# Attention decode with a gated FFN on one core: value loop split per batch, scores moved between transposes, output products in four column groups

## The chip, the core and the metric

One core of a Trainium2 chip runs the whole kernel in one launch. The metric is the device time of that launch in microseconds (us), measured outside the profile; a run's number is the median of several executions. A profile is one further execution with its own time, and its clock starts at zero at the first recorded instruction.

## The reference

Two sequences (B = 2) each decode one token of width 512. The attention part has 32 heads of 128 and a cache of 4096 keys and values per head. A dense two-layer part with 1376 hidden units runs beside it on its own input, and a gate mixes the two results:

```python
q = (x @ wq).reshape(B, 1, 32, 128)               # per head
scores = einsum("bhqd,bhkd->bhqk", q, k) * 128 ** -0.5
p = softmax(scores)
a = (einsum("bhqk,bhkd->bhqd", p, v)).reshape(B, 1, 4096) @ wo
b = relu(B_x @ w1) @ w2
g = sigmoid((x * gate_w).sum(-1))
out = g * a + (1 - g) * b                         # 2 x 512
```

Everything is bf16. The key cache and the value cache are 64 MiB each and every element is used once, so nearly all the bytes that the kernel moves are these two.

## The kernel before, in words

**Tiles.** The caches are cut into 32 pairs: pair i is two heads of one batch, 2 MiB of keys or of values, laid out as 128 partitions x 64 rows x 128. Pairs 0 to 15 belong to batch 0 (`g = 0`), pairs 16 to 31 to batch 1 (`g = 1`). One buffer, `kv_sb`, has four slots for such pairs; load n goes to slot n mod 4. Loads 0 to 31 bring keys, loads 32 to 63 values (V0 to V31 below). SyncE (SP) issues all of them in order (lines 240 to 249). Load n waits until load n - 4 has been used up: for keys until the last transposes of that pair, `T_i_7`, for values until the last product of that pair, `pv_i` (line 244). So V0 to V3 wait for the transposes of key pairs 28 to 31, and V4 waits for `pv_0`. The weights `w1` and `w2` are loaded behind key pair 12, and `wo` in five cuts (16, 8, 4, 2 and 2 of its 32 row blocks) behind the last value pair (`WO_CUTS`, line 250).

**Key stage.** For each pair TensorE (PE) does `T` (lines 314 to 328): 64 transposes of 128 x 128, eight to a PSUM bank, in banks 4 to 7 in turn; the second four groups wait for the banks' copies. VectorE (DVE) and ScalarE (ACT) copy each bank to `kt_sb` (`evac`, lines 343 to 353; DVE five of eight, ACT three). Then `Sc` (lines 330 to 341) multiplies with the queries: 16 matmuls of 512 columns, in four groups of 32 columns of the array (`tile_position`), into the scores of the batch, banks 0 and 1 for `g = 0`, banks 2 and 3 for `g = 1`. `Sc`'s chunks 4 to 7 wait for the copies of this pair that end last. The order on PE is `T`, `Sc`, `T`, `Sc`, in two loops of four turns with four pairs each (lines 360 to 365).

**Softmax.** `row_max` (DVE) and `exps` (ACT) run over all scores of a batch; batch 0's are queued on DVE and ACT among the copies of pairs 17 to 19, batch 1's behind all copies (lines 487 to 498). `ptrans` transposes the exponentials back into the score banks by 64 small PE transposes; `denom` sums the denominators with a matmul and makes `rg` = gate / denominator on DVE.

**Value stage.** `stage_p` (DVE, two copies per pair) puts the weights of a pair into `pst`, four buffers. `PV` (lines 426 to 435) does 64 matmuls of 128 x 128 by two columns per pair, and `o_norm` scales the result. `PV` of pair i waits for its load, its weights and `oT_{i-2}`. One loop of eight turns with four pairs does all 32 (lines 509 to 512).

**Order between.** Behind the key loops PE's queue holds: `ptrans(0)`, `denom(0)`, `ffn_h` (44 matmuls), `ffn_f` (22 matmuls of 256 columns, waiting for `ffn_relu` on ACT and DVE), `ptrans(1)`, `denom(1)`, then the `PV` loop (lines 499 to 512). All of these stand ahead of the first `PV`.

**End.** `o_spread` regroups the attention output, and `proj` multiplies it with `wo`: 32 row blocks by two halves, 64 matmuls of 2 x 256, added onto the FFN's result in banks 6 and 7. DVE and ACT copy one half each, and SP stores 2 x 512 (lines 466 to 485, 519 to 521, 254).

Of the kernel before, what the change touches and what calls it, by code (L numbers as in the profile page):

```python
# [5 lines left out]
ACT = mybir.ActivationFunctionType  # L6
# [8 lines left out]
PER = 4  # L15
NPAIR = 16
NIT = NPAIR // PER
# [119 lines left out]
def bass_gated_mix__gqa_block_cached__dense_activation_relu__decode_kernel(  # L137
# [12 lines left out]
    P = _Prog(nc)  # L150
    f32, b16 = dt.float32, dt.bfloat16
    sb = nc.alloc_sbuf_tensor
# [6 lines left out]
    zt = sb("zt", [128, 512], b16)  # L159
# [29 lines left out]
    out_sb = sb("out_sb", [2, 512], b16)  # L189

    PSF = nc.alloc_psum_tensor("PS", [128, 4096], f32)
    PSB = PSF[:, :].bitcast(b16)
# [1 line left out]
    def bank(b, c0, n, p0=0, p1=128):  # L194
        return PSF[p0:p1, 512 * b + c0:512 * b + c0 + n]
# [44 lines left out]
    for n in range(64):  # L240
        waits = []
# [12 lines left out]
    P.add("sp", lambda e: e.dma_start(out_ap, out_sb[:, :]), waits=["res_0", "res_1"], signal="st", sem="st", inc=16)  # L254
    P.add("sp", lambda e: e.wait_ge(P.sem("st"), 16))


    P.add("pool", lambda e: e.memset(ident16[:], 0.0), signal="c_i0")
# [52 lines left out]
        P.add("dve", fn, waits=["qT", "c_qm"], signal=f"qm_{g}")  # L311


    def T(g, p):
        for q in range(8):
            for rr in range(8):
                r = 8 * q + rr

                def waits(t, q=q):
                    i = NPAIR * g + PER * t + p  # L320
                    w = [f"ld_kv_{i}"] if q == 0 else []
                    if q >= 4:
# [3 lines left out]
                P.add("pe", lambda e, iv, q=q, rr=rr, r=r: e.transpose(bank16(4 + q % 4, rr * 128, 128), kv_sb[:, p, r, :], ident16[:, :]),  # L326
                      waits=waits if rr == 0 else [],
                      signal=(lambda t, q=q: f"T_{NPAIR * g + PER * t + p}_{q}") if rr == 7 else None)

    def Sc(g, p):  # L330
        for c in range(8):
            for hh in range(2):
                def waits(t, c=c):
                    i = NPAIR * g + PER * t + p
                    return ([f"qst_{i}"] if c == 0 else []) + ([f"ev_{i}_{c}"] if c >= 4 else [])

                P.add("pe", lambda e, iv, c=c, hh=hh: e.matmul(  # L337
                    S_chunk(g, c), lhsT=qst[:, p, hh, :], rhs=kt_sb[:, p % NKT, 8 * c:8 * c + 8, 64 * hh:64 * hh + 64],
                    start=False, stop=True, tile_position=(0, 32 * (c % 4)), skip_group_check=True),
                    waits=waits if hh == 0 else [],  # L340
                    signal=(lambda t: f"sc_{NPAIR * g + PER * t + p}") if (c, hh) == (7, 1) else None)
# [17 lines left out]

    for g in range(2):  # L360
        P.begin_loop(NIT)
        for p in range(PER):
            T(g, p)
            Sc(g, p)
        P.end_loop()


    def row_max(g):
        P.add("dve", lambda e: e.tensor_reduce(out=m4[:, g:g + 1], in_=S_region(g), axis=AX.X, op=ALU.max),  # L369
              waits=[f"sc_{NPAIR * g + NPAIR - 1}"], signal=f"m4_{g}")  # L370
        for q in range(4):
            P.add("dve", lambda e, q=q: e.tensor_copy(out=mq[:, g, q:q + 1], in_=m4[32 * q:32 * q + 32, g:g + 1]),  # L372
                  waits=[f"m4_{g}"] if q == 0 else [], signal=f"mq_{g}" if q == 3 else None)
        P.add("dve", lambda e: e.tensor_reduce(out=M32[:, g:g + 1], in_=mq[:, g, :], axis=AX.X, op=ALU.max),
              waits=[f"mq_{g}"], signal=f"M32_{g}")
        for q in range(4):
            P.add("dve", lambda e, q=q: e.tensor_scalar(out=negM[32 * q:32 * q + 32, g:g + 1], in0=M32[:, g:g + 1], scalar1=-1.0,  # L377
                                                        scalar2=None, op0=ALU.mult),
                  waits=[f"M32_{g}"] if q == 0 else [], signal=f"negM_{g}" if q == 3 else None)

    def exps(g):
        P.add("act", lambda e: e.activation(out=E_sb[g][:, :], in_=S_region(g), func=ACT.Exp, bias=negM[:, g:g + 1], scale=1.0,
                                            accum_out=l4[:, g:g + 1]),
              waits=[f"negM_{g}"], signal=f"E_{g}")
# [13 lines left out]
    def denom_l(g):  # L398
        P.add("dve", lambda e: e.tensor_scalar(out=lm[:, g, :], in0=jmask[:, :], scalar1=l4[:, g:g + 1], scalar2=None, op0=ALU.mult),
              waits=[f"E_{g}", "c_j4"], signal=f"lm_{g}")  # L400

    def denom(g):
        P.add("pe", lambda e: e.matmul(bank(MISC, 32 * g, 32), lhsT=ones[:, :], rhs=lm[:, g, :], start=True, stop=True),
              waits=[f"lm_{g}", "c_one"] + (["rg_0", "hTs"] if g else []), signal=f"lb_{g}")
        P.add("dve", lambda e: e.reciprocal(out=rinv[:, g, :], in_=bank(MISC, 32 * g, 32)), waits=[f"lb_{g}"], signal=f"rinv_{g}")  # L405
        P.add("dve", lambda e: e.tensor_scalar(out=rg[:, g, :], in0=rinv[:, g, :], scalar1=g_sb[:, g:g + 1], scalar2=None, op0=ALU.mult),  # L406
              waits=[f"rinv_{g}", "g"], signal=f"rg_{g}")
# [18 lines left out]
    def PV(p):  # L426
        for r in range(64):
            b, blk = p_place(r)

            def waits(t):  # L430
                i = PER * t + p
                return [f"ld_kv_{32 + i}", f"pst_{i}"] + ([f"oT_{i - 2}"] if i >= 2 else [])
            P.add("pe", lambda e, iv, r=r, k=32 * b + blk: e.matmul(o_col(p), lhsT=kv_sb[:, p, r, :], rhs=pst[:, p, k, :],  # L433
                                                                    start=(r == 0), stop=(r == 63)),
                  waits=waits if r == 0 else [], signal=(lambda t: f"pv_{PER * t + p}") if r == 63 else None)


    def ffn_h():
        for ft in range(11):
            n = 128 if ft < 10 else 96  # L440
            for t in range(4):
                P.add("pe", lambda e, ft=ft, t=t, n=n: e.matmul(  # L442
                    bank(MISC, 64 + 2 * ft, 2, 0, n), lhsT=w1_sb[:, t, ft:1280:10] if ft < 10 else w1_sb[:, t, 1280:1376],
                    rhs=xT_sb[:, t, :], start=(t == 0), stop=(t == 3)),
                    waits=["ld_w1", "rg_0"] if ft + t == 0 else [], signal="hT" if (ft, t) == (10, 3) else None)
# [10 lines left out]
    def ffn_f():  # L456
        for ft in range(11):
            n = 128 if ft < 10 else 96
            for a in range(2):
                P.add("pe", lambda e, ft=ft, n=n, a=a: e.matmul(  # L460
                    bank(A_BANKS[a], 0, 256, 0, 2), lhsT=hT_sb[0:n, ft, :], rhs=w2_sb[0:n, ft, 256 * a:256 * a + 256],
                    start=(ft == 0), stop=True, skip_group_check=True),
                    waits=["hTs", "ld_w2a", "ld_w2b"] if ft + a == 0 else [])


    def o_spread():
# [10 lines left out]

    def proj():
        for r in range(32):
            for a in range(2):  # L480
                w = (["os_sb"] if r == 0 else []) + ([f"ld_wo_{WO_CUTS.index(r)}"] if r in WO_CUTS else [])
                P.add("pe", lambda e, r=r, a=a: e.matmul(bank(A_BANKS[a], 0, 256, 0, 2), lhsT=os_sb[:, r, :],  # L482
                                                         rhs=wo_sb[:, r, 256 * a:256 * a + 256], start=False, stop=True,
                                                         skip_group_check=True),
                      waits=w if a == 0 else [], signal=f"proj_{a}" if r == 31 else None)

    for i in range(32):
        stage_q(i)
    for i in range(32):
# [28 lines left out]
    proj()  # L518
    P.add("dve", lambda e: e.tensor_copy(out=out_sb[:, 0:256], in_=bank(A_BANKS[0], 0, 256, 0, 2)), waits=["proj_0"], signal="res_0")  # L519
    P.add("act", lambda e: e.activation(out=out_sb[:, 256:512], in_=bank(A_BANKS[1], 0, 256, 0, 2), func=ACT.Copy),  # L520
          waits=["proj_1"], signal="res_1")

    P.resolve()
    with nc.Block() as block:
# [47 lines left out]
```

## Time and profile before

| | us |
|---|---|
| median of 3 runs | 366.41 (365.51 to 366.51) |
| the profiled execution's own time | 366.51 |
| its span | 365.0 |
| PE busy | 256.1 |
| DVE busy | 134.1 |
| ACT busy | 97.2 |
| mean transfer rate over the span | 399 GB/s |

The span is what the trace covers; the rest of the execution's time lies around it. A view by windows gives for each stretch the busy time of each engine, the granted clock of PE (1.00 is full), the mean busy share of the 16 DMA engines and the rate. The chain of waits follows the end of the program back: at each step to what released it. A timeline row gives start, length, engine, line, operation, and in brackets the idle time before it and what ended it. The first matmul of a pair of keys runs at 17.9 us, the last score at about 190 us, the first value product at 205.2 us, the last at 349.7 us.

### The profile page before, as it was taken

What the parts mean: (1) busy time and instruction counts of PE and PEld (TensorE: products, weight loads), DVE (VectorE), ACT (ScalarE), POOL (GpSimd) and SP (SyncE); (2) the same over time, 40 slices, a digit from 0 to 9 for tenths busy, and PEclk for the clock granted to TensorE, in tenths of its full rate; (3) what the DMA queues carried; (4) which work ended last, traced back from release to release, by engine and by line L of the source; (5) the groups of instructions that cost most, each with busy time, mean ns of one, the idle gap of its engine ahead of it and who ended that gap; (6) DMA issues with size and microseconds to landing.
All of it is one profiled execution on the core that took longest, in us unless ns stands there. A gap on an engine that the chain in (4) does not pass through costs nothing.

```text
span 365.0 us, 10862 instructions
## 1 busy us (share of the span) xinstructions
PE 256.1 (70%) x5028; PEld 211.3 (58%) x5028; DVE 134.1 (37%) x293; ACT 97.2 (27%) x106; POOL 12.0 (3%) x52
## 2 busy tenths in 40 slices
PE   2499999997999999999997844433344443333457
PEld 0487787776786787778775743333333333333345
DVE  1056666664667666666662311011111100110000
ACT  1054564463564765456441000000000000000000
POOL 5000000000000000000000000000000000000000
PEclk9999999999999999999996655555555555555558
DMA  8999999999999999999994299999999999999990
GB/s 345 406 427 427 431 429 425 429 417 417 428 427 425 422 429 431 427 427 429 427 425 208 52 429 431 429 431 426 429 427 425 427 426 431 431 429 427 431 405 15
DMA packets 10505, 145.64 MB, mean 399 GB/s; under 512 B 1173, under 2 KB 1274, under 8 KB 1658
## 3 DMA queue, kind: packets, MB, share of 16 engines
q1 hardware_dynamic: 10484, 145.43, 94.2%
q8 instruction: 10, 0.16, 0.2%
q14 instruction: 5, 0.04, 0.0%
q10 hardware_dynamic: 6, 0.00, 0.0%
HBM read 145.43 MB, written 0.00 MB: 398 GB/s over the span
## 4 chain that ended last, share of the span: by engine, by line
PE 51%; DMA 44%; DVE 2%; issue 1%; SPq 0%; ACT 0%; DVEq 0%
PE PS L326 29%; DMA kv_sb<-in_A_v_cache_dram 28%; PE PS L337 11%; DMA kv_sb<-in_A_k_cache_dram 10%; DMA wo_sb<-in_A_wo_dram 6%; PE PS L433 5%; PE PS L482 3%; PE PS L460 1%; PE PS L442 1%; DVE m L369 1%; DVE kt_sb L353 1%; PE PS L394 0%; DVE mq L372 0%; DVE negM L377 0%; DVE rinv L405 0%
## 5 line engine op out<-in xcount | busy, mean ns | idle before, releaser
L353 DVE COPY kt_sb<-PS 128x1024 bf16<-128x1024 bf16 x160 | 107.6, 690 | 62.2 <-PE PS L326 62.0
L326 PEld LDWEIGHTS PS<-ident,kv_sb 128*128 128x128 bf16 x2048 | 115.7, 98 | 18.5 <-issue 12.3
L326 PE MATMUL PS<-ident,kv_sb 128*128 128x128 bf16 x2048 | 121.4, 221 | 4.7 <-DMA kv_sb<-in_A_k_cache_dram 3.7
L433 PE MATMUL PS<-pst,kv_sb 128*128 128x2 bf16 x2048 | 59.0, 166 | 86.7 <-DMA kv_sb<-in_A_v_cache_dram 83.1
L350 ACT ACTIVATE kt_sb<-PS 128x1024 bf16<-128x1024 bf16 x96 | 91.6, 1024 | 85.2 <-PE PS L326 85.2
L433 PEld LDWEIGHTS PS<-pst,kv_sb 128*128 128x128 bf16 x2048 | 57.1, 104 | 88.7 <-issue 69.4
L422 DVE TENSOR_TENSOR oT<-PS,rg 128x2 bf16<-128x2 f32 x32 | 5.1, 160 | 127.4 <-PE PS L433 127.4
L337 PE MATMUL PS<-kt_sb,qst 128*32 128x512 bf16 x512 | 51.5, 383 | 0.0
L520 ACT ACTIVATE out_sb<-PS 2x256 bf16<-2x256 f32 x1 | 0.4, 372 | 165.9 <-PE PS L482 165.9
L337 PEld LDWEIGHTS PS<-kt_sb,qst 128*32 128x32 bf16 x512 | 17.9, 95 | 21.1 <-DVE kt_sb L353 14.4
L415 DVE COPY pst<-PS 64x64 bf16<-64x64 bf16 x64 | 14.3, 224 | 0.8 <-issue 0.2
L357 POOL COPY qst<-qmask 128x64 bf16<-128x64 bf16 x32 | 7.4, 236 | 156.2 <-PE PS L337 145.3
L482 PE MATMUL PS<-wo_sb,os_sb 128*2 128x256 bf16 x64 | 10.0, 333 | 2.1 <-DMA wo_sb<-in_A_wo_dram 2.1
L482 PEld LDWEIGHTS PS<-wo_sb,os_sb 128*2 128x2 bf16 x64 | 6.5, 102 | 5.4 <-issue 2.2
L304 PE MATMUL PS<-xT_sb,wq_sb 128*128 128x2 bf16 x128 | 3.6, 166 | 3.5 <-DMA wq_sb<-in_A_wq_dram 3.5
L304 PEld LDWEIGHTS PS<-xT_sb,wq_sb 128*128 128x128 bf16 x128 | 3.5, 104 | 3.6 <-DMA wq_sb<-in_A_wq_dram 3.6
L460 PE MATMUL PS<-w_sb,hT_sb 128*2 128x256 bf16 (+1 forms) x22 | 4.7, 405 | 0.6 <-DVE hT_sb L451 0.6
L519 DVE CAST out_sb<-PS 2x256 bf16<-2x256 f32 x1 | 0.4, 412 | 11.7 <-PE PS L482 11.7
L460 PEld LDWEIGHTS PS<-w_sb,hT_sb 128*2 128x2 bf16 (+1 forms) x22 | 2.6, 122 | 2.4 <-DVE hT_sb L451 0.7
L394 PEld LDWEIGHTS PS<-ident,E 32*64 32x64 bf16 x128 | 3.6, 107 | 0.7 <-issue 0.7
L394 PE MATMUL PS<-ident,E 32*64 32x32 bf16 x128 | 3.8, 179 | 0.0
L442 PE MATMUL PS<-xT_sb,w_sb 128*128 128x2 bf16 (+1 forms) x44 | 2.8, 199 | 1.4 <-DVE rg L406 1.4
(49 smaller groups left out, 28.4 us busy)
## 6 DMA issues: line engine op xcount, KB each, us to landing
kv_sb<-in_A_k_cache_dram SPq DMA_DIRECT2D x32, 2048.0 KB, 14.6
kv_sb<-in_A_v_cache_dram SPq DMA_DIRECT2D x32, 2048.0 KB, 17.6
wq_sb<-in_A_wq_dram SPq DMA_DIRECT2D x1, 4096.0 KB, 12.2
wo_sb<-in_A_wo_dram SPq DMA_DIRECT2D x1, 2048.0 KB, 22.1
w_sb<-in_B_w_dram SPq DMA_DIRECT2D x1, 1376.0 KB, 15.8
w_sb<-in_B_w_dram SPq DMA_DIRECT2D x1, 1280.0 KB, 18.8
wo_sb<-in_A_wo_dram SPq DMA_DIRECT2D x1, 1024.0 KB, 24.1
wo_sb<-in_A_wo_dram SPq DMA_DIRECT2D x1, 512.0 KB, 24.9
```

The lines of the kernel that those rows point to most:

```text
L304: P.add("pe", lambda e, h=h, t=t: e.matmul(bank(7, 2 * h, 2), lhsT=wq_sb[:, t, h * 128:(h + 1) * 128], rhs=xT_sb[:, t, :], start=(t == 0), ...
L326: P.add("pe", lambda e, iv, q=q, rr=rr, r=r: e.transpose(bank16(4 + q % 4, rr * 128, 128), kv_sb[:, p, r, :], ident16[:, :]), waits=waits ...
L337: P.add("pe", lambda e, iv, c=c, hh=hh: e.matmul(S_chunk(g, c), lhsT=qst[:, p, hh, :], rhs=kt_sb[:, p % NKT, 8 * c:8 * c + 8, 64 * hh:64 * ...
L350: P.add("act", lambda e, dst=dst, src=src: e.activation(out=dst, in_=src, func=ACT.Copy), waits=w, signal=f"ev_{i}_{q}", sem=f"ev{p}{q}")
L353: P.add("dve", lambda e, dst=dst, src=src: e.tensor_copy(out=dst, in_=src), waits=w, signal=f"ev_{i}_{q}", sem=f"ev{p}{q}")
L357: P.add("pool", lambda e: e.tensor_copy(out=qst[:, p, :, :], in_=qmask[:, 2 * i:2 * i + 2, :]), waits=[f"qm_{i // NPAIR}"] + ([f"sc_{i - P ...
L394: P.add("pe", lambda e, q=q, b=b, blk=blk, src=src: e.transpose(bank16(2 * g + b, 32 * blk, 32, 0, 64), src, ident16[32 * q:32 * q + 32, 3 ...
L415: P.add("dve", lambda e, hh=hh, base=base: e.tensor_copy(out=pst[64 * hh:64 * hh + 64, p, :, hh].rearrange("p (b k) -> p b k", b=2), in_=b ...
L433: P.add("pe", lambda e, iv, r=r, k=32 * b + blk: e.matmul(o_col(p), lhsT=kv_sb[:, p, r, :], rhs=pst[:, p, k, :], start=(r == 0), stop=(r = ...
L442: P.add("pe", lambda e, ft=ft, t=t, n=n: e.matmul(bank(MISC, 64 + 2 * ft, 2, 0, n), lhsT=w1_sb[:, t, ft:1280:10] if ft < 10 else w1_sb[:, ...
L460: P.add("pe", lambda e, ft=ft, n=n, a=a: e.matmul(bank(A_BANKS[a], 0, 256, 0, 2), lhsT=hT_sb[0:n, ft, :], rhs=w2_sb[0:n, ft, 256 * a:256 * ...
L482: P.add("pe", lambda e, r=r, a=a: e.matmul(bank(A_BANKS[a], 0, 256, 0, 2), lhsT=os_sb[:, r, :], rhs=wo_sb[:, r, 256 * a:256 * a + 256], st ...
```

## The change

Four edits, and one that follows from them:

1. **Value loop per batch.** `PV` gets the batch as an argument and runs in two loops of four turns. Behind the key loops PE does `ptrans(0)`, `denom(0)`, a zeroing matmul, and then the value loop of batch 0. Between the two value loops stand `ptrans(1)`, `denom(1)`, `ffn_h` and `ffn_f`. On DVE, `row_max(1)` and `denom_l(1)` stand behind the weights of value pairs 0 and 1; the weights of pairs 16 to 19 stand ahead of `denom(1)`'s DVE part. `ffn_h` waits for `rg_1`.
2. **Scores inside the next pair's transposes.** Within a turn of a key loop, the first two groups of eight transposes of pair i + 1 are issued ahead of `Sc(i)`, the other six behind it. The transposes of the first four groups now wait for the copies that empty their banks (`ev_{i-1}_{q+4}`).
3. **Four column groups.** `ffn_f` and `proj` use four groups of 32 array columns, each for 128 of the 512 outputs: 44 and 128 matmuls of 2 x 128 where there were 22 and 64 of 2 x 256. They add up in one bank, `ACC`, which the zeroing matmul clears.
4. **Result.** One DVE copy of 98 partitions x 128 replaces the two copies, and two stores (SP and ACT, one batch each, four pieces of 128) replace the one.
5. `MISC` moves from bank 5 to bank 7, `ACC` is bank 6.

```diff
-    MISC = 5
-    A_BANKS = (6, 7)
+    MISC, ACC = 7, 6
+
+    def acc(c):
+        return bank(ACC, 0, 128, 32 * c, 32 * c + 2)
...
-    def T(g, p):
-        for q in range(8):
+    def T(g, p, qs):
+        for q in qs:
...
                     if q >= 4:
                         w.append(f"ev_{i}_{q - 4}")
+                    elif p:
+                        w.append(f"ev_{i - 1}_{q + 4}")
...
         P.begin_loop(NIT)
+        T(g, 0, range(8))
         for p in range(PER):
-            T(g, p)
+            if p + 1 < PER:
+                T(g, p + 1, range(2))
             Sc(g, p)
+            if p + 1 < PER:
+                T(g, p + 1, range(2, 8))
         P.end_loop()
...
-            for a in range(2):
+            for c in range(4):
...
+                P.add("pe", lambda e, r=r, c=c: e.matmul(acc(c), lhsT=os_sb[:, r, :], rhs=wo_sb[:, r, 128 * c:128 * c + 128],
+                                                         start=False, stop=True, tile_position=(0, 32 * c), skip_group_check=True),
...
-    row_max(1)
-    exps(1)
     ptrans(0)
     denom(0)
-    ffn_h()
-    ffn_relu()
-    ffn_f()
-    denom_l(1)
-    ptrans(1)
-    denom(1)
+    P.add("pe", lambda e: e.matmul(bank(ACC, 0, 128), lhsT=zt[:, 0:128], rhs=zt[:, 0:128], start=True, stop=True))
     for i in range(PER):
         stage_p(i)
-    P.begin_loop(2 * NIT)
-    for p in range(PER):
-        PV(p)
-    P.end_loop()
-    for i in range(32):
-        o_norm(i)
-        if i + PER < 32:
-            stage_p(i + PER)
+        if i == 1:
+            row_max(1)
+            exps(1)
+            denom_l(1)
+    for g in range(2):
+        if g:
+            ptrans(1)
+            for i in range(PER):
+                stage_p(NPAIR + i)
+            denom(1)
+            ffn_h()
+            ffn_relu()
+            ffn_f()
+        P.begin_loop(NIT)
+        for p in range(PER):
+            PV(g, p)
+        P.end_loop()
+        for i in range(NPAIR * g, NPAIR * g + NPAIR):
+            o_norm(i)
+            if i + PER < NPAIR * (g + 1):
+                stage_p(i + PER)
     o_spread()
     proj()
-    P.add("dve", lambda e: e.tensor_copy(out=out_sb[:, 0:256], in_=bank(A_BANKS[0], 0, 256, 0, 2)), waits=["proj_0"], signal="res_0")
-    P.add("act", lambda e: e.activation(out=out_sb[:, 256:512], in_=bank(A_BANKS[1], 0, 256, 0, 2), func=ACT.Copy),
-          waits=["proj_1"], signal="res_1")
+    P.add("dve", lambda e: e.tensor_copy(out=out_sb[:, :], in_=bank(ACC, 0, 128, 0, 98)), waits=["proj"], signal="res")
+    for b, eng in enumerate(("sp", "act")):
+        P.add(eng, lambda e, b=b: e.dma_start(out_ap[b].rearrange("(c n) -> c n", c=4), out_sb[b:97 + b:32, :]), waits=["res"],
+              signal=f"st_{b}", sem="st", inc=16)
+    P.add("sp", lambda e: e.wait_ge(P.sem("st"), 32))
```

More of the change, by code (lines that the diff above doesn't have):

```diff
@@ L188, in bass_gated_mix__gqa_block_cached__dense_activation_relu__decode_kernel @@
     os_sb = sb("os_sb", [128, 32, 2], b16)
-    out_sb = sb("out_sb", [2, 512], b16)
+    out_sb = sb("out_sb", [98, 128], b16)
     PSF = nc.alloc_psum_tensor("PS", [128, 4096], f32)
@@ L403, in denom @@
         P.add("pe", lambda e: e.matmul(bank(MISC, 32 * g, 32), lhsT=ones[:, :], rhs=lm[:, g, :], start=True, stop=True),
-              waits=[f"lm_{g}", "c_one"] + (["rg_0", "hTs"] if g else []), signal=f"lb_{g}")
+              waits=[f"lm_{g}", "c_one"] + (["rg_0"] if g else []), signal=f"lb_{g}")
         P.add("dve", lambda e: e.reciprocal(out=rinv[:, g, :], in_=bank(MISC, 32 * g, 32)), waits=[f"lb_{g}"], signal=f"rinv_{g}")
@@ L424, in o_norm, with PV @@
               waits=[f"pv_{i}", f"rg_{g}"], signal=f"oT_{i}", sem=f"on{i % PER}")
-    def PV(p):
+    def PV(g, p):
         for r in range(64):
@@ L434, in PV @@
                                                                     start=(r == 0), stop=(r == 63)),
-                  waits=waits if r == 0 else [], signal=(lambda t: f"pv_{PER * t + p}") if r == 63 else None)
+                  waits=waits if r == 0 else [], signal=(lambda t: f"pv_{NPAIR * g + PER * t + p}") if r == 63 else None)
     def ffn_h():
@@ L444, in ffn_h @@
                     rhs=xT_sb[:, t, :], start=(t == 0), stop=(t == 3)),
-                    waits=["ld_w1", "rg_0"] if ft + t == 0 else [], signal="hT" if (ft, t) == (10, 3) else None)
+                    waits=["ld_w1", "rg_1"] if ft + t == 0 else [], signal="hT" if (ft, t) == (10, 3) else None)
     def ffn_relu():
@@ L458, in ffn_f @@
             n = 128 if ft < 10 else 96
-            for a in range(2):
[L460 to L463, printed above, removed]
+            for c in range(4):
+                P.add("pe", lambda e, ft=ft, n=n, c=c: e.matmul(
+                    acc(c), lhsT=hT_sb[0:n, ft, :], rhs=w2_sb[0:n, ft, 128 * c:128 * c + 128], start=False, stop=True,
+                    tile_position=(0, 32 * c), skip_group_check=True),
+                    waits=["hTs", "ld_w2a", "ld_w2b"] if ft + c == 0 else [])
     def o_spread():
@@ L479, in proj @@
         for r in range(32):
-            for a in range(2):
+            for c in range(4):
                 w = (["os_sb"] if r == 0 else []) + ([f"ld_wo_{WO_CUTS.index(r)}"] if r in WO_CUTS else [])
[L482 to L485, printed above, removed]
+                P.add("pe", lambda e, r=r, c=c: e.matmul(acc(c), lhsT=os_sb[:, r, :], rhs=wo_sb[:, r, 128 * c:128 * c + 128],
+                                                         start=False, stop=True, tile_position=(0, 32 * c), skip_group_check=True),
+                      waits=w if c == 0 else [], signal="proj" if (r, c) == (31, 3) else None)
     for i in range(32):
```

4 lines of the change are left out of this document (1 added, 3 removed).

## The prediction

> **What bounds the kernel now.** I read the page first, then the chain of waits, then windows over the stretches that stood out, then single rows. A difference within 0.3% of this time, about 1.1 us, is what a measurement of this kernel can't tell from no change.
>
> ```profile
> span 365.0 us, 10862 instructions
> ...
> PE 51%; DMA 44%; DVE 2%; issue 1%; SPq 0%; ACT 0%; DVEq 0%
> ```
>
> ```profile
> 86.00:91.00 5.00, 2.61 (x36) 1.56 (x31) 1.29 (x3) 0.17 (x2) 0.24 (x1) 1.00 1.02 433
> 180.00:190.00 10.00, 10.00 (x158) 7.96 (x155) 6.73 (x10) 5.71 (x6) 0.00 (x0) 1.00 1.01 427
> 190.00:200.00 10.00, 8.00 (x125) 6.54 (x125) 3.52 (x15) 1.45 (x4) 0.00 (x0) 0.73 0.61 256
> 200.00:210.00 10.00, 8.83 (x257) 7.82 (x256) 3.35 (x16) 0.00 (x0) 0.00 (x0) 0.67 0.21 56
> 220.00:240.00 20.00, 7.41 (x256) 7.15 (x256) 2.10 (x12) 0.00 (x0) 0.00 (x0) 0.50 1.00 428
> ```
>
> The chain gives PE 51%, which invites the reading that PE is the limit of half the kernel. The last three columns of the windows (granted clock, DMA share, GB/s) say otherwise: with PE 100% busy (180 to 190) the loads still run at 427 GB/s, with PE 37% busy (220 to 240) at 428. The loads are the limit in both stages; there are two places where they aren't. One is 190 to 210: at 428 GB/s those 20 us would have carried what now takes 10 x 256/428 + 10 x 56/428 = 7.3 us, so **12.7 us of transfer time is lost there**. The other is the end. The chain shows what fills both:
>
> ```profile
> 188.66 1.55 PE PS L337 x16
> 190.24 1.24 DVE m L369
> ...
> 192.97 0.37 DVE rinv L405
> ...
> 193.75 2.80 PE PS L442 x44
> ...
> 197.15 4.68 PE PS L460 x22
> 201.83 1.82 PE PS L394 x64
> ...
> 205.17 6.59 PE PS L433 x241
> 211.75 2.43 issue
> ...
> 330.53 22.10 DMA wo_sb<-in_A_wo_dram
> 352.76 9.97 PE PS L482 x64
> ```
>
> After the last scores come the second batch's row maximum, the FFN, the second transposes, and only then the first value product, whose end frees a slot. At the end the 64 products with wo take 9.97 us from the landing of their first half.
>
> **The gap in the middle.** When SP gets to issue its loads:
>
> ```profile
> 188.69 0.33 SPq L235 DMA_DIRECT2D kv_sb<-in_A_v_cache_dram  x1
> ```
> ```profile
> 207.07 0.33 SPq L235 DMA_DIRECT2D kv_sb<-in_A_v_cache_dram  x1
> ```
>
> These are V3 (freed by the last key transposes) and V4 (freed by the first value pair): 18.4 us apart. In the window from 190 the rate of 256 over 10 us is 6.0 us of full flow, so the flow ends near 196.0; the 56 of the next window is 1.3 us, so it starts again near 208.7, 1.6 us after V4's issue. To keep the flow whole, V4 must be issued by about 194.4.
>
> Take the worst case first, in which the moved scores win nothing and PE is as late as now. The last scores end at 190.2. In the new order `ptrans(0)` follows at once, then `denom(0)`, two copies of `stage_p`, and the value product. The present kernel shows that very sequence for batch 1: from 201.83 to 205.17, 3.3 us. The zeroing matmul is one PE instruction beside the DVE steps. So the first product starts at 193.6 and, with the length of one pair from the rows below, ends at 195.4: V4 is 1.0 us too late, and 11.7 of the 12.7 us are back.
>
> ```profile
> 342.97 1.84 PE L433 MATMUL PS<-pst,kv_sb 128*128 128x2 bf16 x64 [3.06 <-DMA kv_sb<-in_A_v_cache_dram]
> 347.86 1.84 PE L433 MATMUL PS<-pst,kv_sb 128*128 128x2 bf16 x64 [3.05 <-DMA kv_sb<-in_A_v_cache_dram]
> ```
>
> These rows also give the pace of the loads: 4.89 us per pair of 2 MiB, of which PE works 1.84. What waits behind the moved DVE steps: `row_max(1)` (190.24 to 192.97, 2.7 us with its small steps), the exponentials (1.11 us below) and `denom_l(1)` now stand ahead of the weights of pairs 2 and 3 and of `oT_0`, for which pair 2 waits. That holds pair 2 some 4 us, but pairs 0 and 1 are through, V4 and V5 are issued, and V6 is due only 9.8 us after V4. Nothing is lost.
>
> **The moved scores.** How a pair of keys runs now:
>
> ```profile
> 183.37 0.56 PEld L337 LDWEIGHTS PS<-kt_sb,qst 128*32 128x32 bf16 x14
> 184.37 0.11 PEld L337 LDWEIGHTS PS<-kt_sb,qst 128*32 128x32 bf16 x2 [0.45 <-DVE kt_sb L353]
> 184.91 3.58 PEld L326 LDWEIGHTS PS<-ident,kv_sb 128*128 128x128 bf16 x64 [0.42 <-issue]
> 188.59 0.56 PEld L337 LDWEIGHTS PS<-kt_sb,qst 128*32 128x32 bf16 x14
> ```
> ```profile
> 192.97 1.11 ACT L382 ACTIVATE E<-PS,negM 128x1024 bf16<-128x1024 f32 x1 [4.10 <-DVE negM L377]
> ```
> ```profile
> 204.58 1.94 DVE L415 COPY pst<-PS 64x64 bf16<-64x64 bf16 x8
> ```
>
> From scores to scores is 188.59 - 183.37 = 5.22 us, more than the 4.89 of a load, and 0.45 of it is the wait for the last copy. Two groups of transposes in front of the scores cover that wait: 4.77 us. The last pair of each turn still runs bare, so four pairs take 3 x 4.77 + 5.22 = 19.5 us against 19.6 for four loads. I bound this edit by nothing and by 0.45 per pair and take the upper end, since the wait is shorter than the sixteen transposes (0.9 us) put over it. Key pair 31 is in at about 196.0 - 4 x 4.89 = 176.4, its last transposes at 188.7: PE is 12 us behind the loads. At equal pace it ends some 5 to 8 us behind (one pair's own work, and up to 3 us that `row_max(0)` still takes out of DVE), so V4 is issued near 188 to 191 and is in time. The edit is worth the remaining 1.0 us and no more, because the loads set the key stage's length in either case. **Middle: -12.7.**
>
> **The break between the value loops.** From the end of pair 15's product: `ptrans(1)` 1.8; eight copies of `stage_p` 1.9; `denom(1)`'s two DVE steps and the signal 0.8 (192.97 to 193.75), for which `ffn_h` now waits; `ffn_h`, relu and scaling 3.4 (193.75 to 197.15); `ffn_f` 1.5 (44 at the rate taken below; at most the present 4.7); the product of pair 16, 1.8. Sum 11.3, at most 14.5. In that time SP can't issue V20. But at that moment V16 is 3.06 us from landing and V17 to V19 follow at 4.89: the flow lasts 17.7 us, and V20 is due at 16.1. The slack is 4.8 us, so the whole FFN and the second transposes cost nothing there. If the halt of 2.43 us in the chain at 211.75, at the first turn of the value loop, comes again, 2.4 are left. The value pairs behind catch up at 1.84 each.
>
> **The end.**
>
> ```profile
> wo_sb<-in_A_wo_dram SPq DMA_DIRECT2D x2, 256.0 KB, 25.2
> ```
> ```profile
> L235 SPq DMA_DIRECT2D wo_sb<-in_A_wo_dram x5: 418/432/432, 330.5 to 332.4; - x5
> ```
> ```profile
> 1.20 1.90 PE L281 MATMUL PS<-zt 128*32 128x512 bf16 x16 [1.20 <-DVE zt L276]
> ```
> ```profile
> 362.64 0.41 DVE L519 CAST out_sb<-PS 2x256 bf16<-2x256 f32 x1 [11.71 <-PE PS L482]
> 362.75 0.37 ACT L520 ACTIVATE out_sb<-PS 2x256 bf16<-2x256 f32 x1 [165.93 <-PE PS L482]
> ```
>
> The last cut of wo is issued at 332.4 and lands 25.2 later, at 357.6; the products end at 362.7, so 5.1 us of them trail the loads. Now 64 products at 9.97/64 = 156 ns each become 128 of half the width. If the four column groups run at once, the issue rate binds. Lower bound: the value products, 1.84/64 = 29 ns at a granted clock of 0.50. Zeroing matmuls in the same four groups took 1.90/16 = 119 ns for 512 columns, 30 ns per 128. Weight loads of the scores, 0.56/14 = 40 ns. I take 35 ns; the upper bound is no overlap at all, 78 ns. At 35 ns the 128 take 4.5 us, less than the 4.9 from 352.7 to 357.6 in which the rest of wo arrives, so only the last cut's eight products (0.3 us) trail. Copy: at most the present 0.41. From the copies' end (363.12) to the span's end 1.88 stays; two stores of four short pieces each, on two queues, may cost 0 to 0.5 more, I take 0.2. End: 357.6 + 0.3 + 0.4 + 1.9 + 0.2 = 360.4 in place of 365.0. **End: -4.6.**
>
> [...]
>
> **Sum.** 365.0 - 12.7 - 4.6 = 347.7; around the span lie 366.51 - 365.0 = 1.5 us: **349.2 us**. The profiled execution is 0.1 above the median of the runs, which I leave.
>
> **Rivals.**
> *The column groups don't overlap* (the edit doesn't do what it says): 78 ns each, the end stays as it is, 353.8. For it: each product needs its own weight load, and a wait in one group stands ahead of the others in PE's queue. Against it: the 16 zeroing matmuls.
> *PE stays late*: the moved scores win nothing, because they now stand behind transposes that wait for the next load, or the copies slip. 1.0 us of gap stays: 350.2, up to 351.
> *The break outlasts the queue*: `ffn_f` at its present 4.7 and two halts of 2.43 give 14.5 + 4.9 = 19.4 against 16.1: 3.3 us lost, 352.5. For it: the new value loop and the 128 products are more code than before.
> *Slower: the clock falls in the key stage.* Once PE keeps pace it has nothing queued and waits at every load; in the value stage, where it does that, the clock is 0.50. At half clock a pair takes about 2 x 4.77 = 9.5, 4.7 more than a load. By the worst case above PE may end 11 us behind before the flow breaks, some 4.5 more than its 5 to 8; with the 17.3 us won, the change turns slower from (17.3 + 4.5)/4.7, about five pairs, at half clock. Eight give 349.2 + 8 x 4.7 - 4.5 = 382. Against it: from 86 to 91, with PE busy only 2.61 of 5 us and waiting on a load, the clock stayed at 1.00; the waits to come are a tenth of that.
> [...]
>
> **How the numbers follow.** The forecast 0.62; its own range is 347.6 to 350.4: -0.3 and +0.6 from both ends of the store and of the issue rate, and 1.2 below and 0.6 above for the flow, whose full windows differ by some 0.3% (427 and 428; 433 in a short one), worth about 1 us over 345. No overlap 0.12; PE late 0.13; the break 0.10; the clock 0.02. The range is 347.6 to 353.8: it takes in the first three rivals. All but the clock are faster by over 0.3%: 0.97; the clock is slower: 0.02; 0.01 is left for fewer than five pairs at half clock, ending level.
>
> **What would show it.** Windows: no stretch between 20 us and the last value load under about 415 GB/s. V4 issued less than 14 us after V3. The first value product before 192. Score periods of about 4.8 us where PE isn't waiting, clock 1.00 throughout. Some 10 us without value products at the middle of the value stage, with the rate whole. The 128 products done within 0.6 us of the last wo landing. The forecast is wrong if a rate under 400 GB/s shows at the break, if the products trail wo by more than 2 us, or if the granted clock in the key stage is under 1.

## The result, and the profile after

| | before | after |
|---|---|---|
| median | 366.46 us (4 runs) | 351.10 us (4 runs, 350.98 to 351.21) |
| the profiled execution's own time | 366.51 | 350.98 |
| its span | 365.0 | 349.2 |
| mean transfer rate over the span | 399 GB/s | 417 GB/s |

The ratio is 0.957, with a 95% interval of 0.954 to 0.961: 15.4 us faster. The forecast was 349.2 us and the range 347.6 to 353.8, so the direction and most of the size are right; 1.8 us are missing between the sum (349.2) and the profiled execution (350.98). The median lies above the 347.6 to 350.4 that the forecast gave to its own mechanism. It lies inside the wider range, which had been drawn for three rivals, and none of the three is what happened: that part is luck.

From the page of the changed kernel: the span, and the shares of the chain that ended last.

```profile
span 349.2 us, 11060 instructions
...
DMA 49%; PE 44%; issue 3%; DVE 2%; ACT 1%; SPq 1%; DVEq 0%
```

The windows of the changed kernel, for the stretches that the prediction quoted and for the break between the value loops (the last three columns are the granted clock of PE, the DMA share and GB/s):

```profile
86.00:91.00 5.00, 1.01 (x10) 1.04 (x11) 0.00 (x0) 0.00 (x0) 0.00 (x0) 0.50 1.00 426
180.00:190.00 10.00, 9.65 (x185) 7.66 (x182) 5.53 (x9) 4.38 (x5) 0.00 (x0) 1.00 1.00 426
190.00:200.00 10.00, 6.16 (x227) 6.08 (x228) 6.17 (x29) 1.21 (x2) 0.00 (x0) 0.58 1.01 427
200.00:210.00 10.00, 4.79 (x163) 4.49 (x160) 1.35 (x8) 0.00 (x0) 0.00 (x0) 0.50 1.00 424
220.00:240.00 20.00, 7.38 (x256) 7.16 (x256) 1.62 (x10) 0.00 (x0) 0.00 (x0) 0.50 1.01 428
260.00:280.00 20.00, 13.68 (x375) 13.02 (x374) 4.22 (x21) 0.24 (x2) 0.00 (x0) 0.50 1.01 425
```

190 to 210, where the loads ran at 256 and 56 GB/s, now runs at 427 and 424. The break (260 to 280) doesn't show in the rate. V3 and V4 are issued 6.7 us apart, where it was 18.4:

```profile
185.92 0.33 SPq L237 DMA_DIRECT2D kv_sb<-in_A_v_cache_dram  x1
```
```profile
192.61 0.33 SPq L237 DMA_DIRECT2D kv_sb<-in_A_v_cache_dram  x1
```

The chain of waits, cut to what answers the rows of before:

```profile
187.43 1.82 PE PS L400 x64
...
190.77 3.19 PE PS L439 x116
193.96 3.07 issue
197.04 3.55 PE PS L439 x127
200.58 2.47 issue
...
219.49 18.55 DMA kv_sb<-in_A_v_cache_dram
238.18 1.86 PE PS L439 x64
240.06 17.57 DMA kv_sb<-in_A_v_cache_dram
...
320.83 25.24 DMA wo_sb<-in_A_wo_dram
346.12 0.41 PE PS L488 x7
```

The first value product starts at 190.8, 14.4 us earlier than before, and the products with `wo` end 0.5 us behind the last landing (320.83 + 25.24 = 346.07) in place of 5. Two rows are worth a second look. Between 193.96 and 203.05 PE halts twice, for nothing that the chain names; the trace has a fetch of 16 KB of program at each halt, from 194.53 and from 200.47 on. And of the two DMA steps that lead to the value pairs V11 and V15, one took 18.55 us and the other 17.57: about one microsecond appears there once and isn't given back.

### The profile page after: what moved, and what is told of

It reads as the page before. It is cut to its first block, busy times and chain, and to the rows that moved or that the text cites. A ratio compares the mean times of both kernels' runs of the same rounds, so it can differ in the third digit from the quotient of the medians.

```text
span 349.2 us, 11060 instructions
## 1 busy us (share of the span) xinstructions
PE 239.4 (69%) x5115; PEld 205.1 (59%) x5115; DVE 132.4 (38%) x293; ACT 99.4 (28%) x105; POOL 12.0 (3%) x52
## 4 chain that ended last, share of the span: by engine, by line
DMA 49%; PE 44%; issue 3%; DVE 2%; ACT 1%; SPq 1%; DVEq 0%
DMA kv_sb<-in_A_v_cache_dram 29%; PE PS L328 29%; DMA kv_sb<-in_A_k_cache_dram 13%; PE PS L339 9%; DMA wo_sb<-in_A_wo_dram 7%; PE PS L439 5%; SPq L237 1%; DVE kt_sb L355 1%; ACT kt_sb L352 1%; PE PS L400 1%; ACT L388 0%; ACT E L388 0%; DVE m L375 0%; DVE mq L378 0%; DVE negM L383 0%
## 5 line engine op out<-in xcount | busy, mean ns | idle before, releaser
L328 PEld LDWEIGHTS PS<-ident,kv_sb 128*128 128x128 bf16 x2048 | 117.8, 99 | 26.4 <-issue 22.8
L328 PE MATMUL PS<-ident,kv_sb 128*128 128x128 bf16 x2048 | 124.8, 222 | 11.1 <-DMA kv_sb<-in_A_k_cache_dram 9.0
L355 DVE COPY kt_sb<-PS 128x1024 bf16<-128x1024 bf16 x160 | 105.6, 688 | 61.4 <-PE PS L328 61.2
L352 ACT ACTIVATE kt_sb<-PS 128x1024 bf16<-128x1024 bf16 x96 | 94.2, 1023 | 79.8 <-PE PS L328 79.8
L339 PE MATMUL PS<-kt_sb,qst 128*32 128x512 bf16 x512 | 39.1, 390 | 0.0
L339 PEld LDWEIGHTS PS<-kt_sb,qst 128*32 128x32 bf16 x512 | 13.4, 96 | 12.9 <-DVE kt_sb L355 3.6
L488 PE MATMUL PS<-wo_sb,os_sb 128*2 128x128 bf16 x128 | 4.3, 305 | 3.2 <-DMA wo_sb<-in_A_wo_dram 3.1
L488 PEld LDWEIGHTS PS<-wo_sb,os_sb 128*2 128x2 bf16 x128 | 2.9, 112 | 4.4 <-DMA wo_sb<-in_A_wo_dram 2.2
L388 ACT ACTIVATE E<-PS,negM 128x1024 bf16<-128x1024 f32 x2 | 2.2, 1114 | 7.8 <-DVE negM L383 7.8
L448 PEld LDWEIGHTS PS<-xT_sb,w_sb 128*128 128x128 bf16 (+1 forms) x44 | 2.7, 161 | 2.3 <-issue 2.3
```

Of the source, the lines that this page charges most:

```text
L339: P.add("pe", lambda e, iv, c=c, hh=hh: e.matmul(S_chunk(g, c), lhsT=qst[:, p, hh, :], rhs=kt_sb[:, p % NKT, 8 * c:8 * c + 8, 64 * hh:64 * ...
L352: P.add("act", lambda e, dst=dst, src=src: e.activation(out=dst, in_=src, func=ACT.Copy), waits=w, signal=f"ev_{i}_{q}", sem=f"ev{p}{q}")
L355: P.add("dve", lambda e, dst=dst, src=src: e.tensor_copy(out=dst, in_=src), waits=w, signal=f"ev_{i}_{q}", sem=f"ev{p}{q}")
L448: P.add("pe", lambda e, ft=ft, t=t, n=n: e.matmul(bank(MISC, 64 + 2 * ft, 2, 0, n), lhsT=w1_sb[:, t, ft:1280:10] if ft < 10 else w1_sb[:, ...
L488: P.add("pe", lambda e, r=r, c=c: e.matmul(acc(c), lhsT=os_sb[:, r, :], rhs=wo_sb[:, r, 128 * c:128 * c + 128], start=False, stop=True, ti ...
```

## The experiments

Each edit alone, then the whole without one, then what the first four left open. The kernel before had medians of 366.4 to 366.6 us beside them. In the runs that keep the old halves of `proj` but split the loop, `MISC` is bank 7 and `A_BANKS` is `(6, 0)`, since `o_col` uses banks 4 and 5 while the FFN runs.

**The split alone.**

```diff
-    MISC = 5
-    A_BANKS = (6, 7)
+    MISC = 7
+    A_BANKS = (6, 0)
...
+    for g in range(2):
+        if g:
+            ptrans(1)
...
+            ffn_f()
+        P.begin_loop(NIT)
+        for p in range(PER):
+            PV(g, p)
+        P.end_loop()
```

> The kernel before with the split of the value loop alone (FFN and second transposes between the halves, scores and output products as before). Theory of the flow: only the stretch without loads counts, V4 is issued about 7 us after V3 in place of 18.4, so about 11.5 of the 15.4 us come from this edit: 354.5 to 356. Theory of PE as the limit (its 51% of the chain): PE's work is only reordered, so at most the DVE and ACT waits of the chain go, some 4 us: 362.

Measured: 356.87 us (355.99 to 358.03), ratio 0.974 with 0.969 to 0.978. That is 9.5 us of the 15.4, so the theory of PE as the limit is out: PE's busy time did not fall at all (257.5 us against 256.1). It is 0.9 to 2.4 us short of what the theory of the flow had asked. The windows of this run show where:

```profile
260.00:270.00 10.00, 7.16 (x115) 6.54 (x114) 2.70 (x13) 0.24 (x2) 0.00 (x0) 0.50 1.00 428
270.00:275.00 5.00, 5.00 (x67) 3.22 (x65) 0.00 (x0) 0.00 (x0) 0.00 (x0) 0.62 1.00 423
275.00:280.00 5.00, 5.00 (x196) 4.97 (x192) 1.60 (x9) 0.00 (x0) 0.00 (x0) 0.73 0.81 277
```

At 275 to 280 the rate falls to 277: 5 x (1 - 277/428) = 1.8 us of loads lost, in the break between the value loops. This is the prediction's third rival, and it happens when `ffn_f` keeps its 22 wide products.

**The moved scores alone.**

```diff
...
+        T(g, 0, range(8))
         for p in range(PER):
-            T(g, p)
+            if p + 1 < PER:
+                T(g, p + 1, range(2))
             Sc(g, p)
+            if p + 1 < PER:
+                T(g, p + 1, range(2, 8))
```

> The kernel before with the moved scores alone. Theory of the flow: PE's key stage ends some 2.8 us earlier (185.9 in place of 188.7 in the two profiles), and since the order behind it is unchanged the stretch without loads shrinks by just that: 363.5. Theory of PE as the limit: 24 pairs times 0.45 us, 355.7. If the loads set the key stage and nothing else counts: 366.

Measured: 363.07 us (361.81 to 363.64), ratio 0.990 with 0.986 to 0.993. V3 is issued at 186.0 in place of 188.69, and the time falls by 3.3 us, about as much. PE's shorter key stage counts only by the moment at which it ends.

**The column groups alone.**

```diff
-            for a in range(2):
+            for c in range(4):
...
+                    acc(c), lhsT=hT_sb[0:n, ft, :], rhs=w2_sb[0:n, ft, 128 * c:128 * c + 128], start=False, stop=True,
+                    tile_position=(0, 32 * c), skip_group_check=True),
...
```

> The kernel before with the four column groups and the new stores alone. Theory of the flow: this edit counts twice in the old order, since the FFN's 22 products stand ahead of the first value product: 3.3 us from there (4.7 to 1.3) and 4.4 at the end, less 0.5 to 0.8 for the stores: 359.5. If only the end counts, as the prediction's sum has it: 362.5.

Measured: 361.45 us (361.05 to 362.93), ratio 0.987 with 0.983 to 0.992: between the two expectations. The chain of this run tells why the FFN's part is smaller than expected:

```profile
197.13 1.34 PE PS L460 x44
198.47 2.96 PE PS L394 x64
201.44 0.58 PE PS L403 x2
```

The FFN's products fall from 4.68 to 1.34 us, but the 64 small transposes right behind them take 2.96 in place of 1.82 us. In the kernel before the granted clock came up to 1.00 at 201.5, near the end of the 22 wide products, and stayed there to 204.9, by the clock's record in the trace; with the short ones it stays at 0.50 (the mean from 200 to 210 in this run). Of 3.3 us 2.0 arrive: the first value product starts at 203.18 in place of 205.17.

**The split and the scores, without the column groups.** The changed kernel with the old `ffn_f`, `proj`, copies and store.

> The changed kernel without the column groups and the new stores. Theory of the flow: loads end as in the changed kernel (last value pair near 336.2, first cut of wo near 341.2), then 10 us of products at the old rate: 354.6 to 355.5 us. Theory that the column groups saved little and the end is bound by something else (stores, copies): within 1 us of the changed kernel's 351.1.

Measured: 356.59 us (355.99 to 356.89), ratio 0.972 with 0.969 to 0.976: 5.5 us above the changed kernel, and 1 us above the upper end of what the theory gave for the end alone. The break again:

```profile
259.74 3.03 PE L400 MATMUL PS<-ident,E 32*64 32x32 bf16 x64
262.69 0.64 PE L409 MATMUL PS<-lm,ones 128*128 128x32 f32 x2
265.55 2.79 PE L448 MATMUL PS<-xT_sb,w_sb 128*128 128x2 bf16 x44 [2.22 <-DVE rg L412]
268.95 4.72 PE L466 MATMUL PS<-w_sb,hT_sb 128*2 128x256 bf16 x22 [0.61 <-DVE hT_sb L457]
```
```profile
270.00:275.00 5.00, 5.00 (x74) 3.39 (x73) 0.00 (x0) 0.00 (x0) 0.00 (x0) 0.66 0.89 374
275.00:280.00 5.00, 4.79 (x185) 4.70 (x181) 1.59 (x9) 0.00 (x0) 0.00 (x0) 0.68 0.79 270
```

V20 is issued at 275.39, 15.6 us after the last product of the first loop, and the rate is already falling before that. In the changed kernel the same break is 3.3 us shorter (V20 at 271.93), because `ffn_f` takes 1.34 us:

```profile
259.54 3.03 PE L400 MATMUL PS<-ident,E 32*64 32x32 bf16 x64
262.50 0.64 PE L409 MATMUL PS<-lm,ones 128*128 128x32 f32 x2
265.35 2.79 PE L448 MATMUL PS<-xT_sb,w_sb 128*128 128x2 bf16 x44 [2.22 <-DVE rg L412]
268.76 1.34 PE L466 MATMUL PS<-w_sb,hT_sb 128*2 128x128 bf16 x44 [0.61 <-DVE hT_sb L457]
270.04 2.40 PE L439 MATMUL PS<-pst,kv_sb 128*128 128x2 bf16 x84
```

So the column groups, which the prediction had put at the end of the kernel, also keep the flow whole in the middle: the first cut of `wo` is used from 341.16 on in the changed kernel and from 343.21 on here.

**What the rate doesn't show.** The trace holds 16 completion times for each load, as many as the profile counts DMA engines; it doesn't name the engines, and I take each time as one engine's part, and call the earliest of a load its first engine and the latest its last. The first and the last of the 16, in us, for five loads of four kernels, with the number of 16 KB pieces of program that were fetched (queue q8 of the page):

```
                 fetches  key pair 31       V3                V15               V31               last cut of wo
before              10    176.10 to 178.03  195.81 to 198.16  267.93 to 269.40  346.24 to 347.73  356.24 to 357.69
after               13    176.24 to 178.00  195.82 to 197.90  254.56 to 257.63  332.85 to 336.11  342.84 to 346.07
split and scores    12    176.20 to 178.17  195.77 to 198.02  254.50 to 257.83  336.13 to 338.17  346.11 to 348.14
split alone         12    176.26 to 178.19  195.83 to 197.78  256.00 to 257.88  336.09 to 337.99  346.10 to 347.95
```

Up to V3 all four agree. After that the engines of the changed kernel drift apart: from 2.1 us at V3 to 3.2 at the end. With the last cut of `wo` the first engine is done 13.4 us earlier than before, the last one only 11.6, and a product waits for the last. In the kernel before the spread is smaller behind the lost stretch (2.35 at V3, 1.47 at V15), and so it is behind the break of the run without column groups (3.33 at V15, 2.05 at V31), as it would be if an engine that is behind caught up while the others have nothing to do. With the split alone, which loses loads at both places, it is 1.9 at the end. In the changed kernel the step of 18.55 us in the chain is such a drift: the spread grows from 2.10 to 3.07 with the load that lands next after a fetch at 222. The theory that follows: each fetch of program holds one engine, that engine's later loads land later by so much, and a flow without a pause never gives it back.

The sixteen times, one by one, bear this out. These are the changed kernel's V8 and V9, on both sides of the fetch at 222, in us behind the first part, in order of size:

```
V8   0.00 0.16 0.25 0.31 0.43 0.58 0.70 1.45 1.52 1.53 1.60 1.72 1.74 1.74 1.90 2.10
V9   0.00 0.16 0.26 0.32 0.43 0.59 0.71 1.44 1.54 1.59 1.71 1.74 1.75 1.91 2.08 3.07
```

One time has gone from 1.52 to 3.07, and the other fifteen are where they were to within 0.03. Each of the twelve fetches between 17 and 284 us of the changed kernel does this: within the next two loads one of the sixteen times moves by 1.4 to 1.7 us, and it stays there to within 0.2. The smaller steps beside them, of 0.65 to 1.0, come with the five fetches of 8 KB in queue q14. So what a fetch costs depends on the part that it meets: where that part was early, the kernel loses nothing, and where it was among the last, the end moves.

**More program.** Both value loops written out, the work unchanged.

```diff
-        P.begin_loop(NIT)
-        for p in range(PER):
-            PV(g, p)
+        P.begin_loop(1)
+        for i in range(NPAIR):
+            PV(g, i)
         P.end_loop()
```

> The changed kernel with both value loops written out (one turn of 16 pairs each), so that PE's program is some 3,000 instructions longer and about 12 more 16 KB pieces of it are fetched while the loads run. Theory of the slowest engine (a fetch holds one of the 16 DMA engines about 1.3 us, that engine's later loads all land by so much later, and nothing lets it catch up): the worst engine gets one or two fetches more, the sixteen completions of the last cut of wo spread over 4.5 to 6 us in place of 3.2, and the time is 352.4 to 353.7. Theory of the bytes (0.2 MB more at 428 GB/s, shared by all): spread unchanged, 351.6. If fetches don't matter: 351.1.

Measured: 352.68 us (352.55 to 352.70, 5 runs), 1.6 us above the changed kernel, ratio to before 0.962 with 0.959 to 0.964. The DMA queues on this run's page, and below them the same row of the changed kernel's:

```profile
q8 instruction: 25, 0.41, 0.5%
```
```profile
q8 instruction: 13, 0.21, 0.3%
```

Twelve fetches more, 0.2 MB, which at 428 GB/s and shared by all would be 0.5 us. The last cut of `wo` is done between 342.76 and 347.64: the first engine is where it was (342.84), the last is 1.57 later, and the spread is 4.88 in place of 3.24. That is the theory's case, and it is the whole of the loss. The sixteen times stand near multiples of some 1.5 us behind the first (0 to 0.6, one at 2.8, 4.4 to 4.9).

**Less program.** One value loop; the second transposes and the FFN inside it behind a branch.

```diff
                     for op, ws in zip(it.ops, lin):
+                        if isinstance(op, _At):
+                            with eng.If(iv == op.t):
...
+    P.begin_loop(2 * NIT)
+    for p in range(PER):
+        PV(0, p)
...
+    P.begin_at(NIT - 1)
+    ptrans(1)
...
+    ffn_f()
+    P.end_at()
+    P.end_loop()
```

> The changed kernel with one value loop of eight turns in place of two of four; the second transposes and the FFN stand inside it, behind a branch that is taken in the fourth turn. The order of the work is the same, PE's program is some 520 instructions shorter, so two or three 16 KB fetches fewer fall into the loads. Theory of the slowest engine: spread of the last completions 2 to 3.2 us, time 349.8 to 351.1. Theory of the bytes, and no effect of fetches: 351.0 to 351.1, spread as before. The halts at the first turn of the second loop should be gone in all three.

Measured: 350.97 us (350.71 to 351.02, 5 runs), 0.1 under the changed kernel, which these runs can't tell apart. Eleven fetches in place of 13, but the spread at the end is the same (3.2): here the fetch at 206 already moves one time from 1.7 to 3.3 us behind the first. The count doesn't decide, but which part is met, so the number of fetches says nothing here for or against the theory. The halts of the second loop's first turn are gone (192 products in 5.28 us from 270.19 on), together with the three fetches between 270 and 284 us, and the time didn't care.

**Without the moved scores.** The changed kernel with `T` and `Sc` in the old order.

> The changed kernel without the moved scores. By the prediction's worst case V4 is issued 1.0 us too late: 351.8 to 352.3. If the moved scores are worth their 0.45 us per pair on 24 pairs: 361. If nothing: 351.1.

Measured: 351.89 us (351.30 to 353.24), 0.8 above the changed kernel and inside the expectation. V4's parts are done 1.3 to 1.7 us later than in the changed kernel, the last cut of `wo` 1.8 us later on the first engine but only 0.8 on the last (344.65 to 346.86): the pause draws the sixteen together, from 2.16 us at V3 to 1.41 at V9, so the last pays less for it than the first.

**One store.**

```diff
-    P.add("dve", lambda e: e.tensor_copy(out=out_sb[:, :], in_=bank(ACC, 0, 128, 0, 98)), waits=["proj"], signal="res")
...
+    for c in range(4):
+        if c % 2:
+            P.add("act", lambda e, c=c: e.activation(out=out_sb[:, 128 * c:128 * c + 128], in_=acc(c), func=ACT.Copy),
...
+    P.add("sp", lambda e: e.dma_start(out_ap, out_sb[:, :]), waits=["res_2", "res_3"], signal="st", sem="st", inc=16)
```

> The changed kernel with its result copied onto two partitions by four short copies (DVE and ACT two each) and stored by one transfer on SP, as before the change. From the copy's start to the span's end the changed kernel takes 2.65 us (346.55 to 349.2), the kernel before 2.36 (362.64 to 365.0), and 1.8 against 1.5 us lie around the span. Theory that the two stores of short pieces cost: 0.3 to 0.6 us less than the changed kernel, 350.5 to 350.8. Theory that they don't: the four copies cost 0.1 to 0.2 more, 351.2.

Measured: 350.73 us (350.62 to 350.81, 4 runs), 0.4 under the changed kernel without overlap of the runs. The ends of the two timelines, the changed kernel's first:

```profile
346.55 0.29 DVE L530 CAST out_sb<-PS 98x128 bf16<-98x128 f32 x1 [7.23 <-PE PS L488]
346.87 0.65 SPq L532 DMA_DIRECT2D out_dram<-out_sb  x1
346.88 0.62 ACTq L532 DMA_DIRECT2D out_dram<-out_sb  x1
```
```profile
346.77 0.56 ACT L532 ACTIVATE out_sb<-PS 2x128 bf16<-2x128 f32 x2 [78.40 <-PE PS L488]
346.77 0.59 DVE L535 CAST out_sb<-PS 2x128 bf16<-2x128 f32 x2 [7.24 <-PE PS L488]
347.43 0.32 SPq L537 DMA_DIRECT2D out_dram<-out_sb  x1
```

From the issue to the span's end (349.2 in both) two stores take 2.3 us, one takes 1.8, and the copies are 0.3 longer. Around the span lie 350.81 - 349.2 = 1.6 us, against 1.8.

**Both.** The single value loop and the single store together.

> The changed kernel with both the single value loop and the single store. If the two edits add: 0.4 (store) and 0.1 (loop) under the changed kernel's 351.1, so 350.6. If the slowest DMA engine gets its fetches otherwise than in the two kernels apart, the end moves by one fetch, about 1.4 us, either way: 349.2 or 352. If the value loop's halts matter, which they did not by the windows: below 350.4.

Measured: 350.45 us (350.39 to 351.09, 5 runs), ratio to before 0.956 with 0.954 to 0.958. That is about the sum of the two, 0.65 us under the changed kernel, and the fastest of the kernels here. Of the two edits only the store's gain is clear of the spread of the runs.

## Why the prediction was right, and where it was short

**That the loads bound the kernel** was the step that carried it. The chain gave PE 51%, and the split alone took 9.5 us away without taking any work off PE. The gap closed in the way described: V4 was issued 6.7 us after V3 in place of 18.4, and there is no stretch under 400 GB/s in the windows of the changed kernel above. The lowest of the page's slices between 20 us and the last value load has 411, under the 415 that the prediction had named; it lies at the loads of `w1` and `w2` (79 to 87 us), and was 417 before.

**"Middle: -12.7" is the term that was mis-sized**, and not in the gap itself. The last part of V4 is done at 202.79 and was done at 215.57 before: 12.8 us earlier, and 12.7 in the mean of its sixteen parts. But the last landing of all came only 357.69 - 346.07 = 11.6 us earlier, 1.1 less than the term, and this is the larger part of the 1.8 us that are missing. It is lost behind the gap: 1.0 at V9, after the fetch at 222, and 0.2 at V19 and V20, after those of 276 (8 KB) and 277. In the kernel before, the one fetch of 16 KB behind V4's landing (at 235) met the part that was first, and moved the last by nothing. The prediction took the flow behind the gap as unchanged; it had no term for a fetch of program, and the rate of a window, a mean over 16 engines, doesn't show one. That the drift comes from fetches is shown by the twelve that were added and by the sixteen times on both sides of each; why a fetch goes to the engine that it meets was not found out. The changed kernel's 13 pieces are 0.21 MB in all, and twelve more cost 1.6 us.

**The moved scores** were valued rightly. Their row in the changed kernel:

```profile
177.38 0.56 PEld L339 LDWEIGHTS PS<-kt_sb,qst 128*32 128x32 bf16 x16
178.36 3.58 PEld L328 LDWEIGHTS PS<-ident,kv_sb 128*128 128x128 bf16 x64 [0.42 <-issue]
182.04 0.56 PEld L339 LDWEIGHTS PS<-kt_sb,qst 128*32 128x32 bf16 x16
```

All sixteen weight loads go through without the wait of 0.45, and a pair takes 182.04 - 177.38 = 4.66 us (4.77 forecast). PE ended 185.9 - 178.0 = 7.9 us behind the last key pair (5 to 8 forecast), and the worth inside the whole, 1.0 forecast, was 0.8. Alone it is worth 3.3, since there the end of the key stage still counts in full.

**The break** was forecast at 11.3 us from the last product to the issue of V20, and took 271.93 - 259.61 = 12.3: `ptrans(1)` took 3.03 and not 1.8, because its row (1.82 us from 201.83 in the kernel before) was taken from a stretch at clock 1.00 and the break runs at 0.50. It stayed hidden. But the slack was smaller than the 4.8 us given: without the narrow `ffn_f` the same break, 15.6 us, already lost loads, though V20 was said to be due only at 16.1. That time was reckoned from the landings, and the first engines are done up to 3.3 us before a landing (V15 in that run). The rival of the break was thus nearer than its 0.10, and it is the column groups that kept it away, which the prediction had counted only in its slack.

**"End: -4.6"**: the products went at 1.88/64 = 29 ns, the lower bound and not the 35 taken, and ended 0.46 us behind the last landing (0.3 forecast); the copy took 0.29 (0.41). That nothing overlaps (78 ns each), the first rival, is out. The stores were the part that was too cheap: 2.36 us from the copy to the span's end and 1.78 around the span, where 2.1 and 1.5 had been put: 0.5 us, of which the single store gave back 0.4. The 0.2 us for two stores had no row behind it.

The account of the 1.8 us: 1.2 for the last landing (forecast 344.9), 0.2 for the products behind it, -0.1 for the copy, 0.25 for the stores and 0.25 around the span.

**The clock** did fall in the key stage, at one place. In the windows above 86 to 91 has 0.50, where the kernel before had 1.00:

```profile
89.99 1.86 PE L328 MATMUL PS<-ident,kv_sb 128*128 128x128 bf16 x16 [6.73 <-DMA kv_sb<-in_A_k_cache_dram]
```

PE, now ahead, waits 6.73 us for the loads of `w1` and `w2` to pass (2.39 before), and the sixteen transposes behind take 1.86 us in place of 16/64 x 3.58 = 0.9. Through the wait of 2.39 us the clock held at 1.00, through the one of 6.73 it did not: by the clock's record it fell at 85.8, 2.5 us into that wait, and was back at 96.0. The prediction had named a clock under 1 in the key stage as a sign that it is wrong. The sign came up and the time didn't follow it: PE had the time in hand, and the last parts of key pairs 20 and 31 are done at 124.17 and 178.00, against 124.17 and 178.03 before. So the sign was badly chosen; the loads had to be late too. The short waits for loads and copies elsewhere in the key stage, 1.38 us at the longest (up to 121.10), left the clock at 1.00.

**The sum of the parts** is not the whole: 9.5 + 3.3 + 4.9 = 17.7 us alone against 15.4 together. Scores and split work on the same gap: beside the split the scores are worth nothing that these runs can tell without the column groups (356.87 and 356.59), and 0.8 with them, in place of 3.3. The column groups are worth about 5 us either way (4.9 alone; 5.0 beside the split, from 356.87 to 351.89). Beside what they do at the end, they bring the first value product forward when alone, and shorten the break, where loads were lost, when the loop is split.

## What to carry to other kernels

Where a window with a busy engine and a window with an idle one move the same bytes per microsecond (427 GB/s with PE 100% busy and 428 with 37% here), take the loads as the limit, and reckon an edit by what it does to the moment at which the next load is issued: ask for each step whether it stands ahead of that moment, and move everything else behind it. Cover reckoned from the landing of a load was too long here by the spread of its parts (3.33 us at V15 in the run without column groups), and in the changed kernel, whose flow had no pause left behind V3, the end went by the latest of the 16 completion times (346.07, the first at 342.84) and not by the mean rate. Take the length of a short PE step from a stretch with the clock that it will run at: the 64 small transposes took 1.82 us at 1.00 and 3.03 at 0.50.

## What the runs showed of the hardware that was not expected

- The 16 completion times of a load drifted apart when program was fetched beside it: each of the twelve fetches of 16 KB between 17 and 284 us of the changed kernel put one of them 1.4 to 1.7 us further back, and it stayed there to within 0.2. Their spread went from 0.6 us at the first load to 3.2 us at the end of the changed kernel, and to 4.9 with twelve more fetches. They stayed apart while the loads ran without a pause (3.07 at V9, 3.06 at V15), and drew together in one (from 2.35 to 1.66 us in the lost stretch of the kernel before, V3 to V4).
- Products of 2 x 128 in four column groups went at 29 ns each at half clock (1.88/64), the same as products of 128 x 2 in a whole array (1.84/64). In the kernel before the clock came up 4.4 and 5.8 us after products of 256 columns began to run one behind the other (from 197.15, up at 201.5, and from 352.76, up at 358.5). With the narrow ones it did not, but their bursts (1.34 and 1.88 us) were too short to tell whether it is the shape; of the 128 x 2 products, 6.59 us without a pause (from 205.17, before) left it at 0.50.
- The clock fell without a long wait: in the changed kernel at 191.6, and PE's longest wait since the end of the scores at 187.4 had been 1.1 us. What ran in between were small transposes and the first value products.
- The store of eight short pieces from two queues took 2.3 us from issue to the end, that of two 1 KB rows 1.8: 0.5 us more, and some 0.2 us more that lie outside the span.
